# Attention spans loaded by head halves, W2 in 8 KB runs, and W1's columns read by TensorE at a step of four

## The chip, the cores and the metric

One core of a Trainium2 chip. The metric is the time of one execution on the device in microseconds (us); every figure of a run below is the median of its executions, and a profile is of one of them. In profile lines PE is TensorE, PEld its weight loads, DVE VectorE, ACT ScalarE, POOL GpSimd and SP SyncE (POOL and SP also issue DMAs); a DMA has landed when its data are there.

## The reference

Sliding-window attention with a linear bias, then a normalised MLP with a residual, for 8 sequences of 576 tokens, 8 heads of 64:

```python
scores = q @ k.T / 8 + bias            # window of 128 keys, causal
x = softmax(scores) @ v                # -> (8, 576, 512)
xn = (x - mean(x)) / sqrt(var(x) + 1e-6) * g_ln
out = x + maximum(xn @ w_ch1, 0) @ w_ch2      # 512 -> 2048 -> 512
```

The 4608 rows are 36 blocks of 128. W1 is 512 x 2048, W2 is 2048 x 512, both FP32 in memory and cast to FP16 by the load (each of the four loads of either writes 512 KB in the profiles).

## The kernel before

The kernel is a list of tasks. On the host a list scheduler orders the tasks of every engine from assumed costs, and the order is then emitted; a tile framework looks at what each instruction reads and writes and puts the semaphore waits in. Filler matmuls, whose results nobody uses, run in places where TensorE would idle. The parts that matter (cuts are marked):

```python
w1sb = sb("w1sb", [P, NKB, ffn], FP16)        # 128 x 4 x 2048
w2sb = sb("w2sb", [P, NFB, d_model], FP16)    # 128 x 16 x 512
w1r = moe_w_ch1.rearrange("(kb p) f -> p kb f", p=P)
w2r = moe_w_ch2.rearrange("(fb p) d -> p fb d", p=P)
# ...
W_AFTER = [7, 10, 10, 17, 22, 22, 28, 28]     # when each quarter of W1 and W2 is issued (on POOL)
# quarter m of W1, then of W2:
nc.gpsimd.dma_start(out=w1sb[:, :, 512 * m : 512 * m + 512], in_=w1r[:, :, 512 * m : 512 * m + 512])
nc.gpsimd.dma_start(out=w2sb[:, 4 * m : 4 * m + 4, :], in_=w2r[:, 4 * m : 4 * m + 4, :])
# ...
# one group of the first product (chunk c, 128 hidden features f):
for kb in range(NKB):
    nc.tensor.matmul(fb[b][:, 0:n_], w1sb[:, kb, f * P : f * P + P], xt[c][:, kb, 0:n_],
                     start=(kb == 0), stop=(kb == NKB - 1))
# q and k of two neighbouring blocks (a span) are loaded together, 8 heads at once:
nc.sync.dma_start(out=r[n][:, :, :], in_=src[b, :, s0 : s0 + 2 * P, :].rearrange("h (p t) d -> p h (t d)", t=2))
```

The softmax here doesn't subtract the row's maximum and nothing guards it: scores larger than these inputs give would overflow.

## Time and profile before

| | kernel before |
|---|---|
| median, first set of runs | 319.78 us (319.33 to 322.37) |
| TensorE busy | 311.0 of 320.6 us |
| MLP matmuls | 640 with W1, 592 with W2 |
| first W1 matmul in the profile | 29.35 us |
| W1's quarters landed | 22.3, 29.2, 32.8, 39.5 us |

TensorE is full from 31 us to the end, so the time is the begin of that full stretch plus a fixed amount of work.

### The profile page before, as it was taken

To read this page: it belongs to the slowest core of one execution; us is meant where nothing else is said; L and a number is where in the kernel's file an instruction comes from. 1 tells how busy PE (TensorE), PEld (TensorE's weight loads), DVE (VectorE), ACT (ScalarE), POOL (GpSimd) and SP (SyncE) were. 2 spreads that over 40 slices of the span, in tenths; PEclk is the share of its full clock that TensorE was granted. 3 is DMA by queue.
4 is the path that set the end of the run, shared out by engine and by line. 5 is a ranking of instruction groups with operands and counts; after the bars stand their busy time and mean duration, and the time that the engine had idled before them with its cause. 6 is when DMAs were issued, how large, how long until landed. Compare 5 with 4: busy or idle time off the path is not lost.

```text
span 320.6 us, 6377 instructions
## 1 busy us (share of the span) xinstructions
PE 311.0 (97%) x2547; PEld 168.8 (53%) x2547; DVE 180.9 (56%) x411; ACT 164.1 (51%) x261; POOL 96.1 (30%) x125
## 2 busy tenths in 40 slices
PE   8959999999999999999999999999999999999995
PEld 6747676555555444445454445444445444444453
DVE  4657559963499556755665566546655665221012
ACT  3848985336656752475257525752575257305600
POOL 4436095684257165523432331101100000000000
PEclk9997999999999999999999999999999999999999
DMA  8999999999999999999999999826700220011011
GB/s 190 236 195 214 212 190 188 151 180 179 170 133 193 163 155 151 183 167 161 146 165 152 63 155 165 97 51 131 133 16 18 82 86 16 17 67 65 0 67 65
DMA packets 155344, 41.45 MB, mean 129 GB/s; under 512 B 138289, under 2 KB 150833, under 8 KB 155314
## 3 DMA queue, kind: packets, MB, share of 16 engines
q0 software_dynamic: 92768, 15.34, 67.3%
q1 hardware_dynamic: 62544, 25.70, 41.8%
q8 instruction: 20, 0.33, 0.4%
q14 instruction: 10, 0.08, 0.1%
q10 hardware_dynamic: 2, 0.00, 0.0%
HBM read 36.70 MB, written 9.44 MB: 144 GB/s over the span
## 4 chain that ended last, share of the span: by engine, by line
PE 91%; SPq 4%; DMA 2%; DVE 1%; issue 0%; ACT 0%; ACTq 0%
PE fb L911 39%; PE fb L883 39%; PE sc L701 6%; PE fb L773 5%; SPq L359 3%; DMA k<-in_k_dram 2%; SPq L454 1%; PE fb L834 1%; PE fb L617 1%; PE sc L717 0%; ACT probs L749 0%; PE fb L949 0%; DVE xs L822 0%; DVE ot L919 0%; DVE ht L893 0%
## 5 line engine op out<-in xcount | busy, mean ns | idle before, releaser
L911 PE MATMUL fb<-w2sb,ht 128*128 128x512 f16 (+1 forms) x592 | 135.8, 373 | 0.0
L883 PE MATMUL fb<-xt,w1sb 128*128 128x512 f16 (+2 forms) x640 | 132.9, 358 | 0.1
L895 ACT ACTIVATE ht<-fb 128x512 f16<-128x512 f32 (+2 forms) x141 | 79.6, 566 | 78.5 <-PE fb L883 76.5
L883 PEld LDWEIGHTS <-w1sb 128*128 128x128 f16 x640 | 60.1, 98 | 56.1 <-issue 0.2
L749 ACT ACTIVATE probs<-sc 128x1024 f16<-128x1024 f32 (+1 forms) x72 | 67.1, 972 | 40.6 <-PE sc L701 40.5
L911 PEld LDWEIGHTS <-ht 128*128 128x128 f16 x592 | 54.1, 98 | 55.7
L919 DVE SCALAR_TENSOR_TENSOR ot<-fb,rstd,xb 128x512 f32<-128x512 f32 (+1 forms) x37 | 27.2, 734 | 49.3 <-PE fb L911 48.9
L467 POOL DMA_DIRECT2D vx<-in_v_dram x34 | 28.8, 848 | 71.7 <-PE fb L773 64.1
L756 DVE TENSOR_TENSOR probs<-probs,mreg 128x1024 f16<-128x1024 f16 (+1 forms) x48 | 30.6, 652 | 25.0 <-ACT probs L749 24.8
L773 PEld LDWEIGHTS <-probs 128*128 128x128 f16 x544 | 25.0, 98 | 14.3 <-ACT probs L749 1.3
L467 POOL DMA_DIRECT2D qk<-in_q_dram x30 | 25.3, 845 | 23.4 <-DMA qkt<-qk 11.9
L794 DVE TENSOR_TENSOR xb<-fb,rec 128x256 f16<-128x256 f32 x72 | 30.4, 423 | 2.1
L467 POOL DMA_DIRECT2D qk<-in_k_dram x30 | 25.3, 845 | 10.9 <-DMA vx<-in_v_dram 5.8
L773 PE MATMUL fb<-vx,probs 128*128 128x65 f16 x544 | 27.8, 194 | 0.7 <-ACT probs L749 0.7
L790 DVE RECIPROCAL rec<-fb 128x4 f32<-128x4 f32 x72 | 12.8, 178 | 27.6 <-PE fb L773 27.4
L822 DVE SCALAR_TENSOR_TENSOR xs<-xb,mv,g_t 128x512 f16<-128x512 f16 x36 | 27.1, 752 | 0.9
L811 DVE BATCH_NORM_STATS2 st<-xb 128x6 f32<-128x512 f16 x36 | 25.0, 693 | 1.0
L701 PEld LDWEIGHTS <-qkt 64*128 64x128 f16 x544 | 15.4, 94 | 11.7 <-issue 11.0
L701 PE MATMUL sc<-qkt 64*128 64x128 f16 x288 | 19.8, 218 | 0.0
L701 PE MATMUL sc<-qkt,qkt 64*128 64x128 f16 x256 | 18.5, 220 | 0.0
L893 DVE TENSOR_SCALAR ht<-fb 128x256 f16<-128x256 f32 (+2 forms) x19 | 9.8, 524 | 13.8 <-PE fb L883 13.5
L949 PE MATMUL fb<-warm_t 128*128 128x128 f16 x97 | 8.7, 243 | 1.1 <-DVE warm_t L371 1.1
(61 smaller groups left out, 106.4 us busy)
## 6 DMA issues: line engine op xcount, KB each, us to landing
out_dram<-ot SPq DMA_DIRECT2D x35, 256.0 KB, 2.4
vx<-in_v_dram POOLq DMA_DIRECT2D x28, 128.0 KB, 9.0
qk<-in_q_dram POOLq DMA_DIRECT2D x24, 128.0 KB, 9.6
qk<-in_k_dram POOLq DMA_DIRECT2D x24, 128.0 KB, 9.8
qs<-in_q_dram SPq DMA_DIRECT2D x4, 512.0 KB, 6.1
ks<-in_k_dram SPq DMA_DIRECT2D x4, 512.0 KB, 10.7
w1sb<-in_moe_w_ch_dram POOLq DMA_DIRECT2D x4, 512.0 KB, 11.6
w2sb<-in_moe_w_ch_dram POOLq DMA_DIRECT2D x4, 512.0 KB, 14.2
```

The source lines that it names most:

```text
L467: nc.gpsimd.dma_start(out=dst(p0, n), in_=src[b, :, s0 : s0 + n, :].rearrange("h p d -> p h d"))
L701: nc.tensor.matmul(scs[half][:, g, c0 : c0 + P], kt[rows, 1, hp, :], qkt[i][rows, 0, hp, :], start=not bias, stop=True, skip_group_check=True,
L749: nc.scalar.activation(out=o, in_=n_, func=AF.Exp, scale=inv_sqrt_d)
L756: en.tensor_tensor(out=pv, in0=pv, in1=mask[:, 2 * half : 2 * half + 2, :, lo:], op=ALU.mult)
L773: nc.tensor.matmul(pp[:, hh * (D + 1) : hh * (D + 1) + D + 1], probs[i][:, bank, slot, side * P : side * P + P], vx[i - 1 + side][:, h, 0 ...
L794: nc.vector.tensor_tensor(out=xb[i][:, 256 * half : 256 * half + 256].rearrange("p (h d) -> p h d", d=D), in0=pp[:, :, 0:D], in1=rec[2 * i ...
L811: nc.vector.bn_stats(out=st[i][:, :], in_=xb[i][:, :])
L822: nc.vector.scalar_tensor_tensor(out=xs[i][:, :], in0=xb[i][:, :], scalar=mv[c][:, j, 0:1], in1=g_t[:, :], op0=ALU.subtract, op1=ALU.mult,)
L883: nc.tensor.matmul(fb[b][:, 0:n_], w1sb[:, kb, f * P : f * P + P], xt[c][:, kb, 0:n_], start=(kb == 0), stop=(kb == NKB - 1),)
L895: nc.scalar.activation(out=ht[c][:, f, 0:n_], in_=src, func=AF.Relu)
L911: nc.tensor.matmul(pm[:, 0 : c1 - c0], ht[c][:, f, j * P : j * P + P], w2sb[:, f, c0:c1], start=(f == 0), stop=(f == NFB - 1),)
L919: nc.vector.scalar_tensor_tensor(out=ot[i][:, c0:c1], in0=fb[plan.held[key][1]][:, 0 : c1 - c0], scalar=rstd[c][:, j : j + 1], in1=xb[i][: ...
```

## The change

The intent is an earlier begin: the spans of blocks 0 to 3 come in by halves of the heads, so that scores of four heads can begin before all eight are there, and W2 comes in as one 8 KB run per partition and quarter (four neighbouring rows) in place of four runs of 2 KB. The rows of W2 in a partition then belong to hidden features 4p, 4p+1, 4p+2, 4p+3 of that quarter, so the hidden features must come out of the first product in the same order: TensorE takes W1's columns at a step of four. The schedule's settings were made anew (long tables of engine choices, priorities and holds, cut here).

```diff
-    W_AFTER = [7, 10, 10, 17, 22, 22, 28, 28]
+    W_AFTER = [8, 10, 11, 20, 21, 22, 23, 28]
+    BY_HALVES = [0, 2]
-    w2r = moe_w_ch2.rearrange("(fb p) d -> p fb d", p=P)
+    w2r = moe_w_ch2.rearrange("(m p j) d -> p m (j d)", p=P, j=CB)
+    w1f = w1sb[:, :, :].rearrange("p kb (m c j) -> p kb m j c", c=P, j=CB)
# ... span loads, casts, transposes and evictions by halves of the heads (cut)
-                    nc.gpsimd.dma_start(out=w2sb[:, 4 * m : 4 * m + 4, :], in_=w2r[:, 4 * m : 4 * m + 4, :])
+                    nc.gpsimd.dma_start(out=w2sb[:, 4 * m : 4 * m + 4, :].rearrange("p j d -> p (j d)"), in_=w2r[:, m, :])
-                        fb[b][:, 0:n_], w1sb[:, kb, f * P : f * P + P], xt[c][:, kb, 0:n_],
+                        fb[b][:, 0:n_], w1f[:, kb, f // CB, f % CB, :], xt[c][:, kb, 0:n_],
# ... tables of settings (cut)
```

More of the change, by code (lines that the diff above doesn't have):

```diff
@@ L267 @@
     SPAN = 36.0
-    LEAD = 1.55
-    WARM = 26.0
-    TABLE_AFTER = 3
-    MIX_AFTER = 4
+    LEAD = 1.65
+    WARM = 24.0
+    TABLE_AFTER = 2
+    MIX_AFTER = 3
     SPLIT = 5
@@ L274 @@
     V_CAST = 5
+    BY_HALVES = [0, 2]
     HALVED = []
     SPANS = [0, 2, 5, 7]
-    SLACK = (0, 0.3, 0)
-    PICK = {('xt', 0): 'ACT', ('xt', 8): 'ACT', ('cv', 5): 'POOL', ('cv', 0): 'ACT', ('ev', 8): 'ACT', ('ev', 1): 'DVE', ('ev', 3): 'ACT', ('ck', 8): 'POOL ACT', ('cq', 5): 'POOL', ('ev', 5): 'ACT', ('ck', 2): 'POOL ACT', ('ck', 7): 'POOL ACT', ('cq', 6): 'ACT', ('cq', 2): 'POOL ACT', ('xt', 6): 'DVE', ('cq', 8): 'POOL ACT', ('xt', 5): 'DVE', ('cv', 7): 'ACT', ('cv', 3): 'POOL', ('xt', 3): 'DVE', ('ev00', 4): 'ACT', ('cs1', 1): 'POOL', ('cs0', 0): 'POOL', ('ev10', 3): 'ACT', ('xt', 2): 'DVE', ('cq', 3): 'POOL ACT', ('cs0', 8): 'ACT', ('ev01', 8): 'DVE ACT', ('ev10', 8): 'DVE', ('ev11', 5): 'ACT', ('cs0', 2): 'ACT', ('cq', 4): 'POOL ACT', ('ev00', 8): 'DVE', ('ev01', 0): 'DVE ACT', ('cv', 8): 'POOL ACT', ('ev11', 0): 'ACT', ('cv', 4): 'POOL ACT', ('ev01', 6): 'DVE', ('cv', 6): 'POOL', ('ev10', 5): 'DVE ACT', ('cs1', 4): 'POOL ACT', ('ev', 0): 'DVE ACT', ('cv', 2): 'POOL', ('ev00', 2): 'DVE ACT', ('ev00', 7): 'ACT', ('ev10', 2): 'ACT', ('xt', 1): 'ACT', ('ev11', 8): 'DVE ACT', ('xt', 4): 'ACT', ('ev00', 1): 'ACT', ('cv', 1): 'POOL', ('ev01', 7): 'DVE', ('ev11', 6): 'DVE', ('cq', 1): 'POOL', ('ev01', 4): 'DVE ACT', ('cs0', 5): 'ACT', ('ev', 7): 'ACT', ('xt', 7): 'DVE', ('ev', 9): 'ACT', ('cv', 9): 'POOL', ('cq', 11): 'POOL ACT', ('cs1', 9): 'POOL ACT', ('ev00', 10): 'DVE ACT', ('eva', 5): 'DVE', ('cka', 9): 'POOL ACT', ('cv', 11): 'POOL ACT', ('cqa', 10): 'DVE', ('ckb', 10): 'DVE', ('ck', 10): 'ACT', ('ev00', 5): 'ACT', ('ckb', 3): 'POOL DVE ACT', ('evb', 5): 'DVE ACT', ('ev', 11): 'DVE ACT', ('ev01', 2): 'DVE ACT', ('ckb', 6): 'DVE', ('eva', 11): 'DVE', ('cqb', 7): 'POOL', ('cka', 1): 'DVE', ('ev00', 3): 'ACT', ('cq', 0): 'POOL', ('ev01', 5): 'DVE', ('cqb', 5): 'DVE', ('ev10', 4): 'DVE', ('ev01', 9): 'DVE', ('cqa', 8): 'POOL', ('ev10', 10): 'DVE', ('evb', 4): 'ACT', ('cqb', 8): 'DVE', ('cs0', 9): 'DVE', ('cka', 3): 'DVE', ('cqa', 2): 'ACT', ('cka', 8): 'ACT', ('cqa', 5): 'POOL DVE ACT', ('cq', 7): 'ACT', ('ck', 1): 'POOL', ('cka', 0): 'ACT', ('cqa', 7): 'ACT', ('ev10', 11): 'ACT', ('cqa', 4): 'DVE', ('ev11', 11): 'ACT', ('eva', 10): 'DVE ACT', ('ev11', 4): 'DVE', ('eva', 3): 'DVE ACT', ('ev11', 2): 'DVE', ('cqa', 6): 'DVE', ('cqa', 9): 'POOL ACT', ('cqa', 11): 'POOL', ('ev', 2): 'DVE ACT', ('cs0', 4): 'ACT', ('ckb', 11): 'DVE', ('ckb', 2): 'DVE', ('ck', 5): 'POOL', ('cs1', 8): 'ACT', ('ev01', 10): 'DVE ACT', ('ev', 10): 'ACT', ('cq', 10): 'POOL', ('eva', 4): 'DVE ACT', ('cv', 10): 'POOL', ('ev', 6): 'DVE ACT', ('ck', 11): 'ACT', ('cs1', 11): 'POOL ACT', ('cqb', 1): 'POOL DVE ACT', ('ckb', 7): 'DVE', ('ev11', 1): 'DVE ACT', ('ck', 4): 'ACT', ('cka', 11): 'DVE', ('ckb', 0): 'POOL ACT', ('cs1', 0): 'POOL DVE', ('eva', 7): 'DVE ACT', ('cs0', 11): 'POOL ACT', ('evb', 8): 'DVE ACT', ('ev10', 6): 'DVE', ('eva', 2): 'DVE', ('cqb', 2): 'ACT', ('cq', 9): 'ACT', ('ev10', 9): 'DVE', ('ev10', 0): 'DVE', ('evb', 6): 'DVE', ('eva', 8): 'ACT', ('cqa', 3): 'DVE', ('ck', 9): 'ACT', ('evb', 3): 'DVE ACT', ('cs0', 1): 'POOL DVE', ('cqb', 9): 'POOL ACT', ('cqb', 0): 'DVE', ('evb', 2): 'ACT', ('evb', 1): 'ACT', ('cqb', 6): 'DVE', ('eva', 9): 'DVE ACT', ('evb', 10): 'ACT', ('cqb', 11): 'POOL DVE ACT', ('cka', 10): 'POOL ACT', ('ck', 6): 'ACT', ('ckb', 1): 'POOL', ('ev10', 7): 'ACT', ('cs1', 7): 'POOL', ('ev01', 3): 'DVE ACT', ('cs0', 7): 'POOL', ('cs0', 6): 'POOL DVE', ('cs1', 3): 'ACT', ('cka', 2): 'ACT', ('cqa', 1): 'POOL ACT', ('ev01', 1): 'ACT', ('cs0', 10): 'POOL ACT', ('cka', 4): 'POOL DVE ACT', ('ev00', 6): 'DVE', ('xt', 10): 'DVE', ('cqb', 3): 'DVE', ('evb', 0): 'DVE', ('ev00', 0): 'ACT', ('xt', 9): 'ACT', ('ev11', 7): 'DVE', ('cqb', 4): 'ACT', ('ev00', 9): 'DVE', ('ev00', 11): 'DVE ACT', ('ckb', 9): 'DVE', ('ev11', 3): 'DVE ACT', ('ev01', 11): 'ACT', ('evb', 7): 'ACT', ('ckb', 4): 'POOL ACT', ('ckb', 5): 'DVE', ('cs1', 5): 'ACT', ('cs0', 3): 'ACT', ('cka', 7): 'POOL', ('ev11', 9): 'DVE ACT', ('cka', 5): 'DVE', ('cqb', 10): 'POOL', ('cs1', 6): 'POOL', ('eva', 6): 'DVE ACT', ('cs1', 10): 'POOL ACT', ('eva', 1): 'DVE', ('evb', 9): 'DVE', ('ev10', 1): 'ACT', ('eva', 0): 'DVE ACT', ('cka', 6): 'ACT', ('ev11', 10): 'DVE', ('ev', 4): 'DVE', ('ck', 3): 'POOL'}
@@ L279 @@
-    PRI = {'Sb3': 6.6}
-    HOLD = {'QT9.i': 53.04, 'mkb5': 43.12, 'mmixc': 29.86, 'xs6': 50.81}
+    SLACK = (0, 0.1, 0.1)
+    PICK = {('xt', 0): 'ACT', ('xt', 8): 'DVE', ('cv', 5): 'ACT', ('cv', 0): 'POOL', ('ev', 8): 'ACT', ('ev', 1): 'DVE', ('ev', 3): 'ACT', ('ck', 8): 'POOL ACT', ('cq', 5): 'POOL', ('ev', 5): 'DVE', ('ck', 2): 'POOL', ('ck', 7): 'POOL ACT', ('cq', 6): 'POOL', ('cq', 2): 'POOL ACT', ('xt', 6): 'DVE', ('cq', 8): 'POOL', ('xt', 5): 'DVE', ('cv', 7): 'POOL ACT', ('cv', 3): 'ACT', ('xt', 3): 'DVE', ('ev00', 4): 'ACT', ('cs1', 1): 'DVE', ('cs0', 0): 'POOL', ('ev10', 3): 'ACT', ('xt', 2): 'DVE', ('cq', 3): 'POOL ACT', ('cs0', 8): 'POOL DVE', ('ev01', 8): 'DVE ACT', ('ev10', 8): 'DVE', ('ev11', 5): 'ACT', ('cs0', 2): 'POOL ACT', ('cq', 4): 'POOL', ('ev00', 8): 'DVE', ('ev01', 0): 'DVE ACT', ('cv', 8): 'POOL ACT', ('ev11', 0): 'ACT', ('cv', 4): 'POOL ACT', ('ev01', 6): 'ACT', ('cv', 6): 'POOL', ('ev10', 5): 'DVE ACT', ('cs1', 4): 'POOL ACT', ('ev', 0): 'DVE ACT', ('cv', 2): 'POOL', ('ev00', 2): 'DVE ACT', ('ev00', 7): 'ACT', ('ev10', 2): 'ACT', ('xt', 1): 'ACT DVE', ('ev11', 8): 'DVE', ('xt', 4): 'ACT DVE', ('ev00', 1): 'ACT', ('cv', 1): 'POOL ACT', ('ev01', 7): 'DVE', ('ev11', 6): 'DVE ACT', ('cq', 1): 'POOL', ('ev01', 4): 'DVE ACT', ('cs0', 5): 'POOL', ('ev', 7): 'ACT', ('xt', 7): 'DVE', ('ev', 9): 'ACT', ('cv', 9): 'POOL', ('cq', 11): 'POOL ACT', ('cs1', 9): 'POOL ACT', ('ev00', 10): 'DVE', ('eva', 5): 'ACT', ('cka', 9): 'POOL ACT', ('cv', 11): 'POOL ACT', ('cqa', 10): 'DVE', ('ckb', 10): 'ACT', ('ck', 10): 'ACT', ('ev00', 5): 'ACT', ('ckb', 3): 'POOL', ('evb', 5): 'DVE', ('ev', 11): 'ACT', ('ev01', 2): 'DVE ACT', ('ckb', 6): 'DVE', ('eva', 11): 'DVE ACT', ('cqb', 7): 'ACT', ('cka', 1): 'DVE', ('ev00', 3): 'ACT', ('cq', 0): 'ACT', ('ev01', 5): 'DVE', ('cqb', 5): 'DVE', ('ev10', 4): 'DVE', ('ev01', 9): 'DVE ACT', ('cqa', 8): 'DVE', ('ev10', 10): 'DVE', ('evb', 4): 'DVE ACT', ('cqb', 8): 'POOL ACT', ('cs0', 9): 'DVE', ('cka', 3): 'DVE', ('cqa', 2): 'ACT', ('cka', 8): 'ACT', ('cqa', 5): 'POOL DVE ACT', ('cq', 7): 'POOL', ('ck', 1): 'POOL', ('cka', 0): 'ACT', ('cqa', 7): 'ACT', ('ev10', 11): 'ACT', ('cqa', 4): 'DVE', ('ev11', 11): 'ACT', ('eva', 10): 'ACT', ('ev11', 4): 'DVE', ('eva', 3): 'ACT', ('ev11', 2): 'DVE', ('cqa', 6): 'POOL', ('cqa', 9): 'POOL ACT', ('cqa', 11): 'POOL DVE ACT', ('ev', 2): 'DVE ACT', ('cs0', 4): 'POOL ACT', ('ckb', 11): 'DVE', ('ckb', 2): 'DVE', ('ck', 5): 'POOL', ('cs1', 8): 'ACT', ('ev01', 10): 'DVE ACT', ('ev', 10): 'ACT', ('cq', 10): 'POOL', ('eva', 4): 'DVE ACT', ('cv', 10): 'ACT', ('ev', 6): 'ACT', ('ck', 11): 'ACT', ('cs1', 11): 'POOL ACT', ('cqb', 1): 'DVE', ('ckb', 7): 'DVE', ('ev11', 1): 'DVE ACT', ('ck', 4): 'POOL ACT', ('cka', 11): 'DVE', ('ckb', 0): 'POOL ACT', ('cs1', 0): 'POOL DVE', ('eva', 7): 'DVE', ('cs0', 11): 'POOL ACT', ('evb', 8): 'DVE', ('ev10', 6): 'DVE', ('eva', 2): 'DVE', ('cqb', 2): 'ACT', ('cq', 9): 'POOL ACT', ('ev10', 9): 'DVE', ('ev10', 0): 'DVE', ('evb', 6): 'DVE ACT', ('eva', 8): 'ACT', ('cqa', 3): 'POOL ACT', ('ck', 9): 'ACT', ('evb', 3): 'DVE ACT', ('cs0', 1): 'POOL DVE', ('cqb', 9): 'POOL ACT', ('cqb', 0): 'ACT', ('evb', 2): 'ACT', ('evb', 1): 'ACT', ('cqb', 6): 'DVE', ('eva', 9): 'ACT', ('evb', 10): 'DVE', ('cqb', 11): 'POOL DVE ACT', ('cka', 10): 'POOL', ('ck', 6): 'POOL ACT', ('ckb', 1): 'POOL', ('ev10', 7): 'ACT', ('cs1', 7): 'POOL', ('ev01', 3): 'DVE ACT', ('cs0', 7): 'POOL ACT', ('cs0', 6): 'POOL', ('cs1', 3): 'DVE', ('cka', 2): 'ACT', ('cqa', 1): 'POOL ACT', ('ev01', 1): 'ACT', ('cs0', 10): 'POOL DVE', ('cka', 4): 'ACT', ('ev00', 6): 'DVE', ('xt', 10): 'DVE', ('cqb', 3): 'DVE', ('evb', 0): 'DVE', ('ev00', 0): 'ACT', ('xt', 9): 'ACT', ('ev11', 7): 'DVE', ('cqb', 4): 'POOL', ('ev00', 9): 'DVE', ('ev00', 11): 'DVE ACT', ('ckb', 9): 'POOL', ('ev11', 3): 'DVE ACT', ('ev01', 11): 'DVE ACT', ('evb', 7): 'DVE', ('ckb', 4): 'POOL ACT', ('ckb', 5): 'POOL ACT', ('cs1', 5): 'ACT', ('cs0', 3): 'POOL', ('cka', 7): 'POOL', ('ev11', 9): 'DVE ACT', ('cka', 5): 'DVE', ('cqb', 10): 'POOL', ('cs1', 6): 'POOL', ('eva', 6): 'DVE ACT', ('cs1', 10): 'POOL ACT', ('eva', 1): 'DVE', ('evb', 9): 'DVE ACT', ('ev10', 1): 'ACT', ('eva', 0): 'ACT', ('cka', 6): 'POOL ACT', ('ev11', 10): 'DVE', ('ev', 4): 'ACT', ('ck', 3): 'POOL', ('cs00', 0): 'POOL ACT', ('cs10', 3): 'POOL ACT', ('cs01', 10): 'ACT', ('cs11', 6): 'POOL', ('cs00', 9): 'ACT', ('cs01', 11): 'POOL', ('cs11', 9): 'ACT', ('cs00', 6): 'POOL DVE', ('cs11', 3): 'POOL DVE', ('cs01', 7): 'POOL ACT', ('cs01', 8): 'DVE', ('cs10', 11): 'ACT', ('cs00', 8): 'ACT', ('cqa', 0): 'ACT', ('cs00', 2): 'POOL DVE', ('cs01', 6): 'POOL DVE', ('cs10', 4): 'DVE', ('cs10', 10): 'POOL ACT', ('cs00', 4): 'ACT', ('ck', 0): 'ACT', ('cs11', 5): 'ACT', ('cs11', 2): 'POOL', ('cs11', 8): 'DVE', ('cs01', 1): 'POOL', ('cs01', 4): 'POOL', ('cs00', 1): 'POOL DVE', ('cs11', 0): 'POOL', ('ckb', 8): 'POOL', ('cs10', 9): 'ACT', ('cs01', 9): 'POOL DVE', ('cs00', 10): 'POOL', ('cs01', 2): 'POOL ACT'}
@@ L281 @@
+    PRI = {'T2.0': 1.2, 'A1.2': 9.3, 'exa6': 1.6, 'cv3': -8.1, 'A1.10': 7.1, 'A1.4': 5.5, 'qs1.2.i': -2.5, 'v10.i': -1.4}
+    HOLD = {'mkb5': 43.12, 'mmixc': 29.86, 'rc1.6': 44.96, 'r1.6': 36.05, 'v8.i': 46.02, 'Sa1': 9.83, 'eT2.11': 15.52}
     BY_BIAS = 5
     MASK_AT = 5
-    QK_BY_DMA = 8
+    QK_BY_DMA = 9
     X_BY_DMA = 12
@@ L448, with load_span @@
     tnew += [add("z3", ("DVE", 0.4), z3, tnew[:1], av(MASK_AT, 0.0))]
-    def load_span(name, src, r, n, i, v):
+    def load_span(name, src, r, n, i, v, h0=0, h1=H):
         (_, _, b, s0), = where(i)
@@ L454, in emit @@
             nc.sync.dma_start(
-                out=r[n][:, :, :],
-                in_=src[b, :, s0 : s0 + 2 * P, :].rearrange("h (p t) d -> p h (t d)", t=2),
-            )
-        t, d = plan.transfer(f"{name}{i}", "SP", 0.6, 1.75 if name + str(i) != "qs0" else 2.15, 1.0, emit, (), v)
+                out=r[n][:, h0:h1, :],
+                in_=src[b, h0:h1, s0 : s0 + 2 * P, :].rearrange("h (p t) d -> p h (t d)", t=2),
+            )
+        share = (h1 - h0) / H
+        t, d = plan.transfer(f"{name}{i}", "SP", 0.6, 0.05 + 1.7 * share + (0.4 if name in ("qs", "qs0") and i == 0 else 0.0), share, emit, (), v)
         r.writes(n, t)
@@ L490 @@
             if SPANS[n] == i:
-                span_load[n] = (load_span("qs", q, qs, n, i, vl), load_span("ks", k, ks, n, i, vl + 0.01))
+                cuts = ((0, H // 2), (H // 2, H)) if i in BY_HALVES else ((0, H),)
+                span_load[n] = {}
+                for x, (h0, h1) in enumerate(cuts):
+                    for a, (name, src, r_) in enumerate((("qs", q, qs), ("ks", k, ks))):
+                        tag = f"{name}{x}." if len(cuts) > 1 else name
+                        span_load[n][a, x] = (load_span(tag, src, r_, n, i, vl + 0.004 * x + 0.002 * a, h0, h1), h0, h1)
             loads[i] = (None, None, load_v(i, vl + 0.02))
@@ L526, in emit @@
                 else:
-                    nc.gpsimd.dma_start(out=w2sb[:, 4 * m : 4 * m + 4, :], in_=w2r[:, 4 * m : 4 * m + 4, :])
+                    nc.gpsimd.dma_start(out=w2sb[:, 4 * m : 4 * m + 4, :].rearrange("p j d -> p (j d)"), in_=w2r[:, m, :])
             last = [t_w[n - 1][0]] if n else []
-            t_w[n] = plan.transfer(f"w{n}", "POOL", 0.8, 3.2, 0.0, emit, [casts[at % 3]] + last, av(i, -60.0))
+            t_w[n] = plan.transfer(f"w{n}", "POOL", 0.8, 3.2 if n < 4 else 2.7, 0.0, emit, [casts[at % 3]] + last, av(i, -60.0))
     span_done, pv_done, qkt_part = {}, {}, {}
@@ L599, in attention, with e_c @@
             if SPANS[n] == i:
-                evs = [[], []]
-                for a, r_, w_ in ((0, qs, qs16), (1, ks, ks16)):
-                    key = f"T{i}.{a}"
-                    def e_c(e, b, r_=r_, w_=w_):
-                        dst = w_[n][:, :, :, :].rearrange("p h d t -> p t h d")
-                        src = r_[n][:, :, :].rearrange("p h (t d) -> p t h d", t=2)
+                evs, casts = [[], []], {}
+                for (a, x), (landed, h0, h1) in span_load[n].items():
+                    r_, w_ = ((qs, qs16), (ks, ks16))[a]
+                    def e_c(e, b, r_=r_, w_=w_, n=n, h0=h0, h1=h1):
+                        dst = w_[n][:, h0:h1, :, :].rearrange("p h d t -> p t h d")
+                        src = r_[n][:, h0:h1, :].rearrange("p h (t d) -> p t h d", t=2)
                         if e == "ACT":
@@ L610, in e_c @@
                             (nc.vector if e == "DVE" else nc.gpsimd).tensor_copy(out=dst, in_=src)
-                    cs = add(f"c{key}", pick(f"cs{a}", "POOL", POOL=1.38, ACT=1.4, DVE=0.8), e_c, [span_load[n][a]], av(i, 0.1 * a))
-                    r_.reads(n, cs); w_.writes(n, cs)
-                    def e_t(e, b, w_=w_):
-                        for hp in range(HP):
-                            pair = w_[n][:, 2 * hp : 2 * hp + 2, :, :].rearrange("p h d t -> p (h d t)").bitcast(FP32)
-                            nc.tensor.transpose(fb[b][:, hp * P : hp * P + P], pair, iden32[:, :])
@@ L618, in attention @@
-                    tt = add(key, ("PE", 0.45), e_t, [cs, d_iden32], av(i, 1.0 + 0.01 * a), acq=("fb", key))
-                    w_.reads(n, tt)
+                    f = (h1 - h0) / H
+                    cs = add(
+                        f"cT{i}.{a}{x}", pick(f"cs{a}{x}", "POOL", POOL=0.12 + 1.26 * f, ACT=0.22 + 1.18 * f, DVE=0.1 + 0.7 * f),
+                        e_c, [landed], av(i, 0.1 * a + 0.2 * x),
+                    )
+                    r_.reads(n, cs); w_.writes(n, cs)
+                    for y in range(2) if f == 1 else (x,):
+                        casts[a, y] = cs
@@ new lines, in attention, with e_t @@
+                for x in range(2):
+                    key = f"T{i}.{x}"
+                    def e_t(e, b, x=x, n=n):
+                        for a, w_ in ((0, qs16), (1, ks16)):
+                            for hp in range(2):
+                                h0 = 4 * x + 2 * hp
+                                pair = w_[n][:, h0 : h0 + 2, :, :].rearrange("p h d t -> p (h d t)").bitcast(FP32)
+                                c0 = (2 * a + hp) * P
+                                nc.tensor.transpose(fb[b][:, c0 : c0 + P], pair, iden32[:, :])
+                    tt = add(key, ("PE", 0.45), e_t, [casts[0, x], casts[1, x], d_iden32], av(i, 1.0 + 0.1 * x), acq=("fb", key))
+                    qs16.reads(n, tt); ks16.reads(n, tt)
@@ L620, in attention, with e_ev @@
                     for blk in range(2):
-                        def e_ev(e, b, a=a, blk=blk, key=key):
-                            src = fb[plan.held[key][1]][:, :].bitcast(FP16).rearrange("p (hp c) -> p hp c", hp=HP)[:, :, P * blk : P * blk + P]
-                            dst = qkt[i + blk][:, a, :, :]
+                        def e_ev(e, b, x=x, blk=blk, key=key):
+                            src = fb[plan.held[key][1]][:, :].bitcast(FP16).rearrange("p (a hp c) -> p a hp c", a=2, hp=2)[:, :, :, P * blk : P * blk + P]
+                            dst = qkt[i + blk][:, :, 2 * x : 2 * x + 2, :]
@@ L627, in e_ev @@
                                 nc.scalar.activation(out=dst, in_=src, func=AF.Copy)
-                        ev = add(f"e{key}{blk}", pick(f"ev{a}{blk}", "DVE ACT", DVE=0.42, ACT=0.6), e_ev, [tt] + evs[0][len(evs[1]) :], av(i + blk, 1.2), rel=key)
+                        ev = add(f"e{key}{blk}", pick(f"ev{x}{blk}", "DVE ACT", DVE=0.42, ACT=0.6), e_ev, [tt] + evs[0][len(evs[1]) :], av(i + blk, 1.2 + 0.1 * x), rel=key)
                         qkt.writes(i + blk, ev)
@@ L632, in attention @@
             ev = span_done[n][i - SPANS[n]]
+            qkt_part[i] = [[ev[0]], [ev[1]]]
         elif i in HALVED:
@@ L734, in attention @@
                 z_ = [add(f"Z{tag}{i}", ("PE", (0.87 if r else 0.46) * part), e_z(halves), t_sid + d_dist[kind > 0], av(i, 1.5 + 0.6 * halves[0]), acq=acq)]
-            st_ = add(f"S{tag}{i}", ("PE", 0.19 + (0.45 if r else 0.23) * part), e_s(halves), z_ + qkt_part[i][halves[0]] + prev, av(i, 2.0 + 0.6 * halves[0]), acq=acq)
+            st_ = add(f"S{tag}{i}", ("PE", 0.19 + (0.45 if r else 0.23) * part), e_s(halves), z_ + qkt_part[i][halves[0]] + ([] if r == 0 else qkt_part[i - 1][halves[0]]), av(i, 2.0 + 0.6 * halves[0]), acq=acq)
             qkt.reads(i, st_)
```

## The prediction

> **What bounds the kernel now.** I read the page first (busy shares, then the row of slices), next the chain of waits, then the start of it in fine windows, and last the DMA queues.
>
> ```profile
> PE 311.0 (97%) x2547; PEld 168.8 (53%) x2547; DVE 180.9 (56%) x411; ACT 164.1 (51%) x261; POOL 96.1 (30%) x125
> PE   8959999999999999999999999999999999999995
> PEclk9997999999999999999999999999999999999999
> ```
>
> TensorE is busy 97% of the span, and its only weak slices are the first four (8 us each) and the last. The clock dips once, in the fourth slice. So the question for any change is: does it take TensorE work away, does it slow the stream, or does it make the full stream start earlier?
>
> ```profile
> 15.17 7.42 DMA k<-in_k_dram
> 22.68 0.04 ACT qk L547
> 23.21 1.02 ACT probs L749
> 29.16 0.36 PE fb L773 x8
> 31.37 4.06 PE fb L883 x24
> ...
> 275.36 13.81 PE fb L911 x64
> 289.18 13.81 PE fb L883 x64
> 302.99 13.87 PE fb L911 x80
> ```
>
> This is the chain that ended last, in order of time (start, length, what). Up to 23 us it runs through DMA issues and one load of k; from 31.37 to 316.9 us it is TensorE alone. The late pieces give the pace: 13.81 us for 64 matmuls is 215.8 ns each, for the first product of the MLP (L883, weights from W1) as for the second (L911). After 31.4 us the stream has no hole that I could find beyond about 0.1 us at each change of matmul kind, so what is left to gain lies before it. In the first stretch:
>
> ```profile
> 20.00:23.40 3.40, 0.04 (x1) 0.04 (x2) 0.64 (x1) 0.72 (x2) 0.44 (x1) 1.00 1.20 243
> 23.40:25.00 1.60, 1.08 (x20) 0.70 (x20) 0.27 (x3) 1.30 (x2) 0.00 (x0) 0.94 1.24 245
> 25.00:29.00 4.00, 4.00 (x46) 3.11 (x44) 2.70 (x7) 3.05 (x6) 3.86 (x5) 0.60 1.20 215
> ...
> ACT qk L547 <- DMA k<-in_k_dram: 4.5, 1, 4.5
> PE fb L663 <- ACT qk L547: 3.5, 1, 3.5
> ```
>
> The columns of the windows are PE, PEld, DVE, ACT, POOL, granted clock, DMA share, GB/s. From 20.0 to 23.4 us TensorE does nothing, and in 25 to 29 us it has a clock of 0.60. The wait lines say why: the cast of block 4's k stands at the head of ScalarE's queue, the second half of that k lands only at 22.6 us, and behind the cast the exponentials of block 3 wait although their scores were done at 18.5 us. Why the k was late:
>
> ```profile
> q0 software_dynamic: 469, 0.48, 76.6%
> q1 hardware_dynamic: 520, 0.13, 23.0%
> ```
>
> That is the DMA queues from 17 to 21 us. [...] The load of k had 128 KB left when W1 began.
>
> [...]
>
> **The change, part by part.**
>
> *TensorE's work.* By the instruction order of both kernels, all useful counts are the same: 640 matmuls with W1, 592 with W2, 544 scores, 544 with v, 32 + 8 + 48 transposes, 40 bias. Only the filler[...] goes from 97 to 90 matmuls, 7 x 56 ns = 0.4 us, in idle time. Raising the limit for transposes by DMA from 8 to 9 does nothing: block 8 is in a span in both.
>
> *W1's columns at step four.* A weight load lasts 98 ns in the trace, overlapped. 448 of its 640 users stream 512 columns (215.8 ns), 128 stream 384 (about 162) and 64 stream 256 (about 109). Even at twice 98 ns the first group would hide it. I count 0. A loss of 14 ns on each of the 448 would be 6.3 us; I hold that unlikely.
>
> *W2 as 8 KB runs.* Same bytes (4 x 1 MB read, 512 KB written), 128 long runs in place of 512 of 2 KB for each quarter. In before the quarters land at 45.9, 48.5, 53.6 and 56.9 us, and the first use of W2 is at 49.5 us, with no wait of TensorE for it. So this takes nothing away directly; it allows an earlier start. [...]
>
> *Half-head spans.* The first half of q and of k together are as many bytes as q alone was, which landed at 5.0 us (k at 6.85). Cast of a half on POOL 0.7 (half of 1.33), four transposes 0.45, eviction 0.6, hand-overs 0.3: first scores at about 7.1 in place of 8.86 us. v lands at 8.05 as before, so the first product with v comes at about 9.0 in place of 9.97: 1 us of lead. All loads up to k of block 4 carry the same bytes, so k still decides; the lead is lost in that wait unless work can be pulled in front of it.
>
> *The reordering that comes along.* This is what I expect to pay. The cast of block 4's k moves from ScalarE to POOL, so block 3's exponentials no longer stand behind it. In before, after 23.36 us come block 3's two exponentials, its products with v, and all of block 4, and the MLP begins at 29.35 us. In after, the order puts only this behind k: cast on POOL 0.96 (what q's cast took) from 22.6 to 23.6; 8 transposes to about 24.2; eviction 1.02 to 25.4; 16 scores, on a halved clock about 1.0, to 26.5; 15 filler matmuls, 0.84 warm or 1.6 cold: the first W1 matmul at 27.5 to 28.3 us, say 28.0.
>
> *The sum.* At 31.37 us before has done two W1 groups (0.65 each), both products of block 4 with v, and the transpose of block 3. After, once begun, does one group, the transpose (0.23) and both products (0.5), 1.38 us. Equal progress is then reached if it begins at 31.37 - 0.65 - 1.38 = 29.34 us. Beginning at 28.0 saves 1.3 us.
>
> **The rivals.**
>
> *k lands early.* If the second half of k gets ahead of W1's first packets, it lands near 18.5 us and everything moves 4 us. For: the race was lost by some 0.6 us of issue time (issued 15.17, W1 at 14.93), and the issue sequence on SP is cut differently now. Against: bytes and W1's trigger (the cast of block 2's v, landed at 14.05) are the same. The gain is then capped by W1: its second quarter landed at 29.18 us and its third at 32.79; the fifth W1 group is 3.3 us behind the first, so a begin before 25.9 only waits: at most 3.4 us, 316.4.
>
> *The supply takes it back.* W1's last quarter is issued in after behind a cast that waits for the q of blocks 5 and 6 (landed 29.0), near 30.4 in place of 26.6 us; it landed at 39.5 and may slip to 42.5. Its first user stands 14 us of TensorE work behind the first W1 matmul, thus at 42.0. So 0 to 1 us could be lost here, and the whole gain if it slips further: 319 to 320. The first W2 matmul is 19.3 us behind the first W1 one, 47.3 us, against a landing of 45.9: enough.
>
> *The strided weight loads show.* Then the late 64-matmul piece with W1 is longer than 13.81 us, and the time 325 or so. [...]
>
> **Range and chances.** Working and cap give 1.3 and 3.4 us. The parameters of the schedule were evidently tuned anew for this version (many single holds and priorities changed), which speaks for a little more than the lower one; I take 2.0: 317.8 us. The low end, 315.4, is the cap plus 1 us for pieces that I could not follow (filler, a shorter cold stretch). The high end, 319.7, is the gain lost to W1's last quarter. Over 2% faster needs 313.4, 3 us beyond the cap: 0.05. Over 2% slower needs the strided loads to show: 0.03.
>
> **What would show it.** Right: ScalarE has no 4.5 us wait for k; POOL has it; first W1 matmul at 27 to 29 us; the late W1 piece still 13.81 us for 64; TensorE full from there on. Wrong: a gap of TensorE over 1 us after 30 us (supply), a first W1 matmul before 26 us (k won its race), or a W1 matmul pace above 216 ns.

The sum is the median of 319.8 us less 2.0, 317.8 us, and the step of four counts 0. From 17 to 21 us W1's loads (q0) moved 469 packets of about 1 KB and the loads issued on SP (q1), the second half of k among them, 520 of about 256 B; q1 had 23.0% of the engines and moved 0.13 MB.

## The result, and the profile after

The changed kernel takes 335.81 us (334.37 to 336.12, four runs) against 319.91 for the kernel before. The ratio is 1.0473, 95% interval 1.041 to 1.0535. A ratio here is the mean time of one kernel's runs over that of the other's of the same rounds, so not quite the ratio of the medians quoted.

The page of the changed kernel, busy line, the two rows of slices (8.3 us each) and the group of W1's matmuls (its last two fields are idle time of TensorE just before them and what ended it):

```profile
PE 317.0 (95%) x2540; PEld 179.9 (54%) x2540; DVE 183.5 (55%) x412; ACT 157.5 (47%) x256; POOL 101.1 (30%) x133
PE   8993859999999999999999999999999999999996
PEclk9997859999999999999999999999999999999999
L903 PE MATMUL fb<-xt,w1sb 128*128 128x512 f16 (+2 forms) x640 | 137.2, 366 | 11.3 <-DMA w1sb<-in_moe_w_ch_dram 11.1
```

The loss is in slices four to six: two holes in TensorE's row and, from the first of them on, a lower clock. The group line names what ended 11.1 us of idle time: loads of W1. The chain of waits says the same, and that the rest of the kernel is as it was (the late 64 matmuls with W1 still take 13.81 us):

```profile
12.98 4.47 DMA q<-in_q_dram
19.81 11.60 DMA w1sb<-in_moe_w_ch_dram
40.08 5.36 DMA w1sb<-in_moe_w_ch_dram
...
287.98 13.81 PE fb L931 x64
301.79 13.81 PE fb L903 x64
```

TensorE's timeline shows the two holes, in brackets the idle time before an instruction:

```profile
25.58 0.33 PE L903 MATMUL fb<-xt,w1sb 128*128 128x384 f16 x1
31.55 1.12 PE L903 MATMUL fb<-xt,w1sb 128*128 128x384 f16 x3 [5.64 <-DMA w1sb<-in_moe_w_ch_dram]
...
45.48 0.83 PE L903 MATMUL fb<-xt,w1sb 128*128 128x256 f16 x3 [5.47 <-DMA w1sb<-in_moe_w_ch_dram]
```

For comparison, the kernel before in its profile: the first W1 matmuls, without a hole, and the issue of W1's last quarter, without a wait:

```profile
29.35 1.46 PE L883 MATMUL fb<-xt,w1sb 128*128 128x384 f16 x8
26.57 0.76 POOL L525 DMA_DIRECT2D w1sb<-in_moe_w_ch_dram  x1
```

The MLP of the changed kernel did begin early, at 25.58 us. One matmul ran, and the second of the same group then stood until 31.55 us. In the trace W1's quarters landed at 20.87, 27.68, 31.41 and 45.44 us. The second matmul needs only the first quarter, which was there; what it waited for is the third. POOL's timeline shows the other half:

```profile
24.74 1.36 POOL L618 CAST qs<-qs 128x1024 f16<-128x1024 f32 x1
40.08 0.75 POOL L533 DMA_DIRECT2D w1sb<-in_moe_w_ch_dram  x1 [13.98 <-PE fb L903]
```

The issue of W1's last quarter waited 14 us for TensorE to run matmuls with W1, although nothing had yet read that quarter. The waits are in the program as built, where they can be read without a chip. DMASW0, 1, 2 and so on are the semaphores that tell of the landing of DMAs issued on POOL. W1's weight loads that wait for W1's DMAs, and the held-back DMA issue, changed kernel:

```
Ldweights w1sb            [waits DMASW0]            # kb = 0: first quarter
Ldweights w1sb            [waits DMASW2, DMASW1]    # kb = 1: second and third quarter
DMACopy w1sb (4th)        [waits PE]
Ldweights w1sb            [waits DMASW5]            # 34th load, kb = 1, first quarter's columns: waits for the fourth
```

The last line is the second hole: the load that waits there reads columns of the first quarter. The first user of the last quarter stands much later, at the 85th W1 weight load (in e1 and e2 below, which have the same order on TensorE, that is the load that waits). In the kernel before, the second quarter is waited for by the fifth group alone, and the DMA of the last quarter waits for nothing:

```
Ldweights w1sb (group 0)  [waits DMASW0]
Ldweights w1sb (group 4)  [waits DMASW1]
Ldweights w1sb (group 8)  [waits DMASW2]
DMACopy w1sb (4th)
```

The windows give the clock that followed (columns: start and end of the window, its length, busy time of PE, PEld, DVE, ACT, POOL, granted clock, DMA share, GB/s):

```profile
25.00:29.00 4.00, 0.90 (x15) 0.63 (x12) 1.57 (x3) 2.87 (x6) 1.09 (x1) 1.00 1.18 212
29.00:32.00 3.00, 0.45 (x2) 0.30 (x3) 0.00 (x0) 0.00 (x0) 0.00 (x0) 0.52 1.40 212
32.00:35.00 3.00, 3.00 (x27) 2.07 (x25) 1.96 (x7) 0.00 (x0) 0.00 (x0) 0.50 1.48 212
40.00:50.00 10.00, 4.53 (x19) 2.57 (x19) 0.79 (x3) 1.80 (x5) 9.93 (x12) 0.66 1.03 159
```

After each hole about 4 us of matmuls ran at half pace (384-column matmuls 320 ns apart in place of 162, from 31.6 to 35.7 and from 45.5 to 49.5 us), which loses some 2 us each. The account: 5.6 + 5.5 us of holes and 2 + 2 us of half clock are 15.1 us, against a measured loss of 15.9.

### The profile page after: what moved, and what is told of

Same layout as the page of the kernel before. It is cut to its first block, busy times and chain, and to the rows that moved or that the text cites. A ratio compares the mean times of both kernels' runs of the same rounds, so it can differ in the third digit from the quotient of the medians.

```text
span 332.7 us, 6339 instructions
## 1 busy us (share of the span) xinstructions
PE 317.0 (95%) x2540; PEld 179.9 (54%) x2540; DVE 183.5 (55%) x412; ACT 157.5 (47%) x256; POOL 101.1 (30%) x133
## 4 chain that ended last, share of the span: by engine, by line
PE 87%; DMA 6%; SPq 3%; DVE 1%; POOL 1%; issue 0%; POOLq 0%
PE fb L903 39%; PE fb L931 37%; DMA w1sb<-in_moe_w_ch_dram 5%; PE sc L721 5%; PE fb L793 5%; SPq L361 2%; SPq L456 2%; DMA q<-in_q_dram 1%; DVE ot L939 1%; PE fb L854 1%; PE fb L636 1%; POOL qk L557 0%; POOL w1sb L533 0%; DVE xs L842 0%; DVE xb L814 0%
## 5 line engine op out<-in xcount | busy, mean ns | idle before, releaser
L903 PE MATMUL fb<-xt,w1sb 128*128 128x512 f16 (+2 forms) x640 | 137.2, 366 | 11.3 <-DMA w1sb<-in_moe_w_ch_dram 11.1
L915 ACT ACTIVATE ht<-fb 128x512 f16<-128x512 f32 (+2 forms) x142 | 78.4, 557 | 79.4 <-PE fb L903 77.7
L903 PEld LDWEIGHTS <-w1sb 128*128 128x128 f16 x640 | 69.8, 115 | 61.7 <-issue 8.8
L793 PE MATMUL fb<-vx,probs 128*128 128x65 f16 x544 | 28.6, 195 | 0.1
L842 DVE SCALAR_TENSOR_TENSOR xs<-xb,mv,g_t 128x512 f16<-128x512 f16 x36 | 27.9, 776 | 1.0
L721 PEld LDWEIGHTS <-qkt 64*128 64x128 f16 x544 | 15.3, 94 | 12.1 <-issue 11.1
L721 PE MATMUL sc<-qkt 64*128 64x128 f16 x288 | 20.1, 218 | 0.0
L913 DVE TENSOR_SCALAR ht<-fb 128x512 f16<-128x512 f32 (+2 forms) x18 | 11.1, 617 | 13.2 <-PE fb L903 13.0
L644 DVE COPY qkt<-fb 128x512 f16<-128x512 f16 x9 | 3.6, 412 | 19.5 <-PE fb L636 14.7
```

Of the source, the lines that this page charges most:

```text
L721: nc.tensor.matmul(scs[half][:, g, c0 : c0 + P], kt[rows, 1, hp, :], qkt[i][rows, 0, hp, :], start=not bias, stop=True, skip_group_check=True,
L793: nc.tensor.matmul(pp[:, hh * (D + 1) : hh * (D + 1) + D + 1], probs[i][:, bank, slot, side * P : side * P + P], vx[i - 1 + side][:, h, 0 ...
L842: nc.vector.scalar_tensor_tensor(out=xs[i][:, :], in0=xb[i][:, :], scalar=mv[c][:, j, 0:1], in1=g_t[:, :], op0=ALU.subtract, op1=ALU.mult,)
L903: nc.tensor.matmul(fb[b][:, 0:n_], w1f[:, kb, f // CB, f % CB, :], xt[c][:, kb, 0:n_], start=(kb == 0), stop=(kb == NKB - 1),)
L915: nc.scalar.activation(out=ht[c][:, f, 0:n_], in_=src, func=AF.Relu)
```

## The experiments

**Theory F, false waits.** Reading W1 at a step makes the framework see overlaps that are not there. In the tile of 128 x 4 x 2048, quarter m is four pieces of 512 columns, one in each kb; from its first to its last column it spans columns of all other quarters. An order rule that compares first-to-last extents for stepped reads would give exactly the waits above (the read with kb = 0 ends before the second quarter's extent begins and waits for the first alone). The rule itself I did not look up; the experiments test what follows from it. **Theory S**: the stepped weight loads are slow (their mean is 115 ns in the profile after, 98 before). **Theory Q**: the new order on POOL issues W1 too late, whatever the waits.

### e1_regrouped: the same change without the false overlap

```diff
-    w1sb = sb("w1sb", [P, NKB, ffn], FP16)
+    w1sb = sb("w1sb", [P, CB, NKB, ffn // CB], FP16)
-    w1f = w1sb[:, :, :].rearrange("p kb (m c j) -> p kb m j c", c=P, j=CB)
+    w1f = w1sb[:, :, :, :].rearrange("p m kb (c j) -> p kb m j c", c=P, j=CB)
-    ... out=w1sb[:, :, 512 * m : 512 * m + 512] ...
+    ... out=w1sb[:, m, :, :] ...
```

> The changed kernel with W1's tile laid out quarter by quarter, so that one load fills one unbroken stretch of each partition; the weight loads keep their step of four, W2 its 8 KB runs. Theory F (false waits: reading W1's columns at a step makes the framework order the second weight load behind W1's second and third quarter, and the last quarter's load behind matmuls): both holes of TensorE (5.6 us at 25.9, 5.5 us at 40.0) and most of the clock at half go; the first W1 matmul stays near 25 us; 315.5 to 317.5 us, so faster than the kernel before. Theory S (the strided weight loads themselves cost, mean 115 ns in place of 98): stays above 330. Theory Q (W1's quarters are issued too late by the new order on POOL, whatever the waits): one hole of several us stays, 321 or more.

Measured: 321.38 us (319.64 to 322.55), before 321.85 in the same rounds, ratio 0.9993 (0.9926 to 1.0061). The built program has the four right waits, and in TensorE's timeline the 5.6 us hole at 26 us has shrunk to one of 0.94 us, which ends with VectorE and not with a load of W1, and there is a small one at 41:

```profile
25.58 0.81 PE L903 MATMUL fb<-xt,w1sb 128*128 128x384 f16 x4
27.34 0.40 PE L854 MATMUL fb<-iden,xs 128*128 128x128 f16 x4 [0.94 <-DVE xs L842]
...
41.56 1.66 PE L903 MATMUL fb<-xt,w1sb 128*128 128x384 f16 x9 [0.35 <-DMA w1sb<-in_moe_w_ch_dram]
```

The whole regression is gone with one layout of one tile, with the step and the 8 KB runs in place. Theory S falls as its cause. By the time alone theory Q would fit (321 or more); but its hole of several us is not there. And 321.4 is not the 315.5 to 317.5 that I expected: the early begin is worth less than I reckoned (below).

### e2_plain_weights: the change without its weight layouts

```diff
-    w2r = moe_w_ch2.rearrange("(m p j) d -> p m (j d)", p=P, j=CB)
-    w1f = ...
+    w2r = moe_w_ch2.rearrange("(fb p) d -> p fb d", p=P)
# ... W2's load as in the kernel before (cut)
-    ... w1f[:, kb, f // CB, f % CB, :] ...
+    ... w1sb[:, kb, f * P : f * P + P] ...
```

> The changed kernel with both weight layouts of the kernel before (W1 read without a step, W2 in 2 KB runs). Theory F: within 1 us of e1_regrouped, 315.5 to 317.5. Theory S: much faster than e1_regrouped. Theory Q: 321 or more, as e1_regrouped.

Measured: 319.47 us (318.93 to 320.63), ratio 0.9950 (0.9883 to 1.0018). Theory Q falls: the new order runs without a regression. It is 1.9 us below e1_regrouped, more than the 1 us I had allowed; the intervals overlap. Part of it is chance: two of e1's four executions (322.27 and 322.55) have a granted clock of 0.993 and 0.995, all four of e2 have 1.0 (see e10 below).

### e3_before_strided and e4_before_regrouped: the layouts alone on the kernel before

The first has only the weight layouts of the diff above; the second has the regrouped tile besides.

> The kernel before with nothing but the two weight layouts changed (step of four, 8 KB runs, one tile). Theory F: the second weight load of the MLP waits for the third quarter (landed 32.8 in before, against a first W1 matmul at 29.4), a hole of 3 us, and the last quarter's load waits for matmuls, another hole of about 5 us: 327 to 334. Theory S: slower by what the weight loads cost, in every chunk of the MLP, without holes. Theory Q: within 1 us of the kernel before.

Measured: 335.22 us (333.90 to 336.72), ratio 1.0430 (1.0365 to 1.0495): a little worse than my 327 to 334. TensorE and POOL in its timeline:

```profile
32.52 2.40 PE L884 MATMUL fb<-xt,w1sb 128*128 128x384 f16 x7 [7.29 <-DMA w1sb<-in_moe_w_ch_dram]
42.70 2.75 PE L884 MATMUL fb<-xt,w1sb 128*128 128x384 f16 x8 [5.66 <-DMA w1sb<-in_moe_w_ch_dram]
...
37.18 0.75 POOL L526 DMA_DIRECT2D w1sb<-in_moe_w_ch_dram  x1 [12.50 <-PE fb L884]
```

The same two holes in the old order. The first is 7.3 us and not the 3 I expected, because the MLP began at 24.9 us here and not at 29.4.

> As e3_before_strided, with W1's tile laid out quarter by quarter. Theory F: the same as the kernel before within 1 us (319 to 321), or up to 1 us better where the 8 KB runs help. Theory S: as slow as e3_before_strided.

Measured: 321.70 us (319.55 to 323.16), ratio 1.0002 (0.9928 to 1.0076). So 4.3% of the time hangs on how one tile is laid out, and the step with the 8 KB runs is otherwise neither gain nor loss within 0.8%. Its profiled run also shows what I had misread in the profile of before:

```profile
20.00:23.40 3.40, 3.40 (x63) 2.86 (x62) 3.11 (x10) 2.84 (x5) 0.36 (x2) 1.00 1.26 249
```

With the order of before, TensorE was full where the profile of before had shown 0.04 us of work: here k landed at 19.28 and the first W1 matmul ran at 25.44 us.

### e5_last_quarter_apart: one of the two false waits alone

```diff
-    w1sb = sb("w1sb", [P, NKB, ffn], FP16)
+    w1sb = sb("w1sb", [P, NKB, ffn - ffn // CB], FP16)
+    w1last = sb("w1last", [P, NKB, ffn // CB], FP16)     # loads and reads of the last quarter go here
```

> The changed kernel with only the last quarter of W1 in a tile of its own, the first three quarters still in one tile. Built, the second weight load still waits for quarters two and three, and the last quarter's load waits for no matmul. If the two holes are two separate false waits: the first hole (5.6 us, and some 2 us of half clock after it) stays, the second goes with its half clock: 335.8 less 7 to 8, 327 to 329 us. If the wait on the landing alone were the cause, 334 or more; if the held-back issue alone, 322 or less.

Measured: 326.62 us (325.29 to 326.96), ratio 1.0206 (1.0174 to 1.0238), just under the range. The first hole is there as before, the second is not:

```profile
24.77 0.33 PE L905 MATMUL fb<-xt,w1sb 128*128 128x384 f16 x1
30.66 1.12 PE L905 MATMUL fb<-xt,w1sb 128*128 128x384 f16 x3 [5.56 <-DMA w1sb<-in_moe_w_ch_dram]
```

The ratios 1.0473, 1.0206 and 0.9993 share the loss out: 2.7% (8.5 us at 320) for the held-back issue of the last quarter with the weight load that waits for it, 2.1% (6.8 us) for the wait on quarters two and three; by the intervals each is good to some 2 us.

### Where the earlier begin went

In e1, e2 and e4 the first W1 matmul ran near 25.5 us, 3.9 us before that of the profile of before, with spans of 317.2 to 318.8 against 320.6. Where did the rest go? "The race" below is whether block 4's k lands early or is long in transfer beside W1's first quarter (in the profile of before, from 17 to 21 us, W1's queue moved 469 packets and 0.48 MB, that of k 520 packets and 0.13 MB; how an engine divides its time between the two is not shown). k landed at 18.0 to 19.7 us in eleven of the fourteen profiles kept, the changed kernel's among them, and at 21.4 to 22.6 us in those of before, e1 and e7. Several runs look for the rest; no version after e2 was faster than it.

**e6_no_halves** (e2 with `BY_HALVES = []`)

> As e2_plain_weights (plain weight layouts, new order), with the spans of blocks 0 to 3 loaded whole. If the halves carry the small gain of e2_plain_weights (0.5 per cent below the kernel before): no better than the kernel before, 320 to 322. If the gain comes from the new order, ScalarE no longer held by the cast of block 4's k: within 1 us of e2_plain_weights, 318.5 to 320.5.

Measured: 321.00 us (320.77 to 323.36), ratio 1.0038 (1.0008 to 1.0068), in the first of the two cases. It points to the halves as what helps in e2, but its schedule differs in more than the halves (the scheduler reorders around them), so I call it suggested, not shown.

**e7_w1_behind_k** (e1 with `W_AFTER = [9, 10, 11, 17, 21, 22, 23, 28]`)

> As e1_regrouped, with W1's first load triggered later and its last earlier[...]. If the loss of the race between k and W1 makes the slow runs of e1_regrouped (319.6 to 322.6): all runs under 320, k landing near 18.5 us every time. If W1's supply is the limit: the first W1 matmul waits, 320 to 323.

Measured: 324.89 us (323.19 to 325.84), ratio 1.0144. The edit missed its aim, to have k landed before W1's first load: the new trigger came as early as the old one (W1 issued at 15.08 us), k landed at 21.41, and the second quarter was issued at 22.02 in place of 18.94 us. It landed at 31.28 us, and TensorE had eight holes of 0.2 to 1.0 us between 26 and 64 us. It says nothing on the race. Later W1 quarters go with 1.4% more time here, but none of these holes ends with a landing of W1 (they end with VectorE and ScalarE), so how they cost is not shown.

**e9_plain_w1_last_early** (e2 with `W_AFTER[3] = 17`)

> As e2_plain_weights, with the last quarter of W1 issued one load of v earlier, ahead of the cast that waits for the spans of blocks 5 and 6. If the slip of that quarter (landed 40.3 us in e2_plain_weights and 41.5 in e1_regrouped) costs, 317 to 319; if nothing waits for it, the same as e2_plain_weights within 0.7 us (318.8 to 320.2).

Measured: 319.97 us (319.28 to 321.32), ratio 0.9998 (0.9972 to 1.0024): no gain. The quarter landed at 39.32, 1 us sooner than in e2, but the scheduler, told of the earlier issue, put its first user earlier too (the 77th W1 weight load in place of the 85th), and TensorE waited 1.9 us for it, until 39.4.

**e10_before_k_first** (kernel before; the order of SP alone is edited after the scheduler)

```diff
     order = plan.run()
+    early = [x for x in order if x[0].name in ("q4.i", "k4.i")]
+    order = [x for x in order if x[0].name not in ("q4.i", "k4.i")]
+    at = [x[0].name for x in order].index("v3.i")
+    order[at:at] = early
```

> The kernel before with one thing moved: on SP the loads of block 4's q and k are issued ahead of block 3's v; every other engine's order is the same. Race theory (the kernel before has two kinds of runs, 319.2 to 320.0 and 321.7 to 322.8 us, as k lands before or behind W1's first quarter): k lands by 18.5 us in the profile, the idle stretch at 20 us is gone, all runs in the lower kind, median 318.5 to 320. Rival (the spread has another source): runs up to 322.8 stay.

Measured: 320.70 us (320.05 to 321.39, six runs), ratio 1.0005 (0.9966 to 1.0044); the eleven runs of before beside it go from 319.15 to 322.88. k landed at 18.0 us and the MLP began at 25.67. None of the six runs is above 321.5, against three of eleven (six runs without one could be chance: 0.15), but none is below 320 either, which I had not expected. The record has a firmer sign. Of the 29 runs of the kernel before beside these experiments the eight above 321.5 us have a granted clock of 0.989 to 0.995, the other 21 (up to 320.83) 0.997 or more; e10's six have 0.998 or more. The profile of before, a run of the slow kind at 0.995, has 3.4 us at half clock behind its hole at 20 us, 0.5% of its span. So the slow kind fits a hole like that one; that it is k's race every time is not shown. e2, e11 and e12 (new order, plain layouts) have no run of this kind among 16.

The timeline of e10 shows two new waits:

```profile
25.46 0.37 PE L773 MATMUL fb<-vx,probs 128*128 128x65 f16 x7 [1.47 <-POOL vx L582]
...
39.93 1.31 PE L883 MATMUL fb<-xt,w1sb 128*128 128x384 f16 x7 [1.34 <-DMA w1sb<-in_moe_w_ch_dram]
```

The second is part of the answer to where the early begin goes: W1's last quarter lands at 39.9 us, and a TensorE that begins 4 us earlier reaches it before it is there. With two shorter waits for W1 (0.41 and 0.20 us) that takes back 1.95 of the 3.7 us. So the begin and W1's supply bound the same stretch, one right behind the other. It is not the whole answer: the profile of e2 waits for W1 nowhere, and its span is 3.4 us shorter than that of before.

**e11_plain_k_first** and **e13_strided_k_first** (the same edit in e2 and in e4), and **e12_plain_again** (e2 once more)

> The same move in e2_plain_weights (new order, half-head spans, plain weight layouts). If the new order is worth anything beyond a better chance in that race: over 0.3 per cent faster than e10_before_k_first, about 318. If not: the same as e10_before_k_first within 0.3 per cent.

Measured: 319.80 us (319.29 to 320.06), ratio 0.9975 (0.9936 to 1.0013), 0.3% under e10_before_k_first: on the line that I had drawn, so undecided.

> The same move in e4_before_regrouped (order of before, W1 at a step of four in a tile laid out by quarters, W2 in 8 KB runs): what the layouts cost or bring without false waits and without the race. If the stepped weight loads (114 ns in place of 98) hide behind the matmuls: the same as e10_before_k_first within 0.3 per cent, or a little faster if the 8 KB runs bring W2 sooner. If they show: slower by 1 us or more.

Measured: 321.71 us (320.45 to 321.87), ratio 1.0033 (0.999 to 1.0075), 1 us over e10_before_k_first in the same rounds by the medians, 0.28% by the ratios, within the 0.3% that I had allowed. With e1 and e2 (1.9 us by the medians, 0.43% by the ratios, part of it the slow kind) this hints that the layouts cost a few tenths of a per cent even without false waits; it is not shown.

> e2_plain_weights once more, with more rounds. If it beats the kernel before: ratio 0.992 to 0.998 again with an interval below 1. If its first result was chance in the race: 0.998 to 1.002.

Measured: 319.92 us (319.27 to 320.62), ratio 0.9980 (0.9941 to 1.0019). The sign is that of the first time, the interval still includes 1. No version beats the kernel before beyond doubt; e2 is the best and ties with it.

## Why the prediction was wrong

**The step that failed.** Under "W1's columns at step four" I wrote "I count 0", and weighed the step only by how long a weight load lasts. What the step changed was what the load waits for, and what the load of W1's last quarter waits for. It cost 4.7% in the changed kernel (e1 against it) and 4.3% alone on the kernel before (e3 against e4). The waits stood in the built program, which could be listed before any run; I compared counts and order there and not waits. My rival "the strided weight loads show" gave the right sign, and 325 us, a third of the loss, with the wrong mechanism. Two of my signs of being wrong came (a gap of TensorE over 1 us after 30 us, a first W1 matmul before 26 us), but I had put the first down to W1's supply alone.

**The weight load itself: right within what the runs resolve.** It became longer, as these two lines of the tile's views show (minimum, median and maximum in ns), kernel before first and the changed one second:

```profile
L883 PEld LDWEIGHTS <-w1sb x640: 95/98/99, 29.3 to 302.4; 128*128 128x128 f16 x160
```

```profile
L903 PEld LDWEIGHTS <-w1sb x640: 110/113/152, 25.5 to 315.0; 128*128 128x128 f16 x160
```

But 64 matmuls of 512 columns still take 13.81 us, and from start to start of neighbouring W1 matmuls the medians of e1 (stepped) and e2 (plain) agree: 216 ns for 512 columns in both, 163 and 162.5 for 384, 109 for 256 in both.

**W2's 8 KB runs: right as far as seen.** W2's second quarter landed 2.6 us behind the first in before, 2.5 us after. No run has them alone; with the step, e4 comes to 1.0002.

**The half-head spans: right, where TensorE's clock is the same.** I expected first scores at 7.1 us in place of 8.86. The profile of e12_plain_again has them at 6.97 and the first product with v at 9.14 (expected 9.0). In the profile of the changed kernel they come at 8.95 and the product at 11.85, but there TensorE ran at half pace until about 12 us, and in the profile of before only until about 4. When the full clock begins changes from run to run, with and without halves (the first clock record lies between 4.3 and 12.0 us in the traces that hold one). Like must be compared with like: where it begins by 4.8 us, first scores come at 6.97 us with halves (e12) against 8.86 and 8.83 without (before, e10); where it begins after 8.8 us, at 8.92 to 8.95 with halves (the changed kernel, e1, e5, e7, e9, e11) against 10.5 to 11.5 without (e3, e4, e6, e13). The granted clock of the views does not tell where the trace has no clock record: it reads 1.00 from 4 to 12 us of the changed kernel, whose first record, of full clock, begins at 12.04 us; and the trace of e2 has no clock record at all, though the two FP32 matmuls shown here took 2.07 us there too. The pace shows in these, the matmuls that spread the norm's gain, before and after (1.24 and 2.07 us):

```profile
4.06 1.24 PE L410 MATMUL fb<-ot,ot 1*128 1x512 f32 x2
```

```profile
4.06 2.07 PE L412 MATMUL fb<-ot,ot 1*128 1x512 f32 x2
```

**"The reordering that comes along. This is what I expect to pay": wrong in size.** ScalarE is indeed free of the cast of k. But the 4.5 us that it stood there in the profile of before were one outcome of a race between k and W1's first quarter: with the same order k landed at 18.7 us in e3 and 19.3 in e4, and the MLP began at 24.9 and 25.4 us. I took a chance loss for the kernel's habit, from a profile of the slowest of three executions (322.4 against 319.3 and 319.8), and took the gain off the median of 319.8. The order itself does shorten the way: in e1, where k landed late (21.6 us), the MLP began 4.0 us behind k, in e7 with its other triggers 5.4, against 6.8 in the profile of before; I had reckoned 5.4.

**"k lands early": it did**, at 18.06 us in the profile of the changed kernel, first W1 matmul at 25.58. That was luck: in e1, the same order, it landed at 21.62. The cap of 3.4 us is just what the profile of e2 shows against that of before (spans of 317.2 and 320.6). The fault was to take it off a median of 319.8, of executions that by their times (319.3 and 319.8) mostly had no such loss; and part of it can go to the next point.

**"The supply takes it back": seen, in part.** In e1 the last quarter landed at 41.5 us and TensorE waited 0.4 us; it waited 1.3 in e10, 1.7 in e12 and not at all in e2. My path to it was off: the quarter was issued at 26.7 us in e1, not near 30.4, since the q before it landed at 24.6 and not at 29.0. (A slip without effect: from the first W1 matmul to the first W2 one the profile of before has 20.1 us, not 19.3.) Without the false waits the whole change comes to 0.9993, and without its weight layouts to 0.995 and 0.998, where I had 0.994.

What stays open: the framework's rule (that it compares extents is inferred from the waits it put in, not looked up), whether the stepped layouts cost a few tenths of a per cent by themselves, what the halves are worth in the whole time, and the full cause of the spread of 319.2 to 322.9 us in the kernel before.

## What to carry to other kernels

When an access pattern changes from a contiguous slice to a stepped one, list the waits of the built program before and after, not only the instructions: the framework can put a dependency between parts of a tile that never touch. Lay a tile out so that each load fills one unbroken stretch of it, or give each load its own tile. And before reading a wait in a profile as the kernel's habit, check which of the executions was profiled, and whether a sibling with the same order shows the wait too.
